# Forty-two matmuls whose result nobody reads, put between the attention scores of units 1 to 7

## The chip, the cores and the metric

The kernel runs on one core of one Trainium2 chip. The metric is the device time of one execution in microseconds: the median of repeated runs. Before the change it is 859.24 us, the median of 3 runs (858.91 to 859.52).

## The reference, cut to what matters

Three stages follow each other: attention with a window of 128 keys and 4 sink keys, a feed-forward block with SoLU and layer norm ("moe1"), and a mixture of 8 experts of which each token takes one ("moe2").

```python
# attention: B, H, S, D = 4, 8, 768, 64
scores = np.matmul(q, k.transpose(0, 1, 3, 2)) / np.sqrt(D)
scores = np.where(is_sink | in_window, scores, -1e9)
a = softmax(scores); x = a @ v                    # to 3072 tokens x 512
# moe1: w_in 512x1024, w_out 1024x512
h = x @ w_in; solu = h * softmax(h); ln = layernorm(solu) * g_ln
x = ln @ w_out
# moe2: logits = x @ w_gate; each token goes to its argmax expert e
out = gate * (relu(x @ w1[e]) @ w2[e])
```

## The kernel before, in words

Attention is cut into 32 **units** (n = 0 to 31): two heads by half a sequence each, in three blocks of 128 queries. Line numbers are those of the kernel before. `a_scores(n)` makes six score tiles `s` of 128 x 272 on TensorE (L220 with plain fp32 operands for units 0 to 2, the pair L223 and L224 from unit 3 on). Each is read by VectorE (L226: adds the mask `mk`, takes the row's extreme `mx`) and then by ScalarE (L228: exponential into `P`). After the six, VectorE and GpSimd make the normalised weights `pk`; `a_trans` transposes them on TensorE (L281, tile `tp`), ScalarE copies them out (L282, `pt`), and `a_out` multiplies them with the values (L297 and L303, tile `av`; L308 and L309 copy the result to `bxh` and `bxl`). `a_sinks` handles the sink keys (`skp`).

The weights `w_in` and `w_out` arrive as 64-bit words and are decoded in the first 110 us in 16 **pieces**. A piece is a DMA into `w` on ScalarE's queue, work on VectorE (L329 `dt`, L331 `dec`, L336 `dh`), ScalarE (L332, L334), one add on GpSimd (L335), and a split into a high and a low part (L344 and L345 for `w_in`: `wih`, `wil`; L373 and L374 for `w_out`). A piece of `w_out` also goes through TensorE (L353 `wt`, L361 `wt2`).

moe1 then takes tiles of 128 tokens: `m_in` makes `h` in two halves of twelve matmuls of 512 columns (L433 to L435), `m_act` applies SoLU and the norm, `m_tr` transposes (`lt`), `m_out` makes `x2` (L498 to L500).

PSUM has eight buffers, in two groups: three for the attention tiles `s`, `tp`, `skp`, `av`, and five for the rest (`h`, `lt`, `x2`, the decode's `dt`, `dh`, `wt`, `wt2` and some more). A buffer is given to a new tile only when the tile before it has been read for the last time. The text of the program gives each step a priority; a scheduler then lays down a fixed order of instructions for each engine, and each engine works through its own order strictly in turn.

Of the kernel before, what the change touches and what calls it, by code (L numbers as in the profile page):

```python
# [10 lines left out]
BF16 = mybir.dt.bfloat16  # L11
# [19 lines left out]
WB, DB, EB, NXR, XGB = 3, 4, 2, 2, 6  # L31
PA = 3
NATP = 3
KLV = 2
HWP = 3
LA = 2
# [12 lines left out]
def raw(ap):  # L49
    return ap.bitcast(F32)  # L50
# [3 lines left out]
def body(ctx, tc, a):  # L54
    nc = tc.nc
    V, A, G, T, SY = nc.vector, nc.scalar, nc.gpsimd, nc.tensor, nc.sync
    qT, kx, vp, vk = a["qT"], a["kx"], a["vp"], a["vk"]

    const = ctx.enter_context(tc.tile_pool(name="const", bufs=1))
# [18 lines left out]
    def ps(name):  # L78
        if name in ATT:
            a_ = True  # L80
        elif name in MOE:
            a_ = False
        else:
            flip[0] += 1
            a_ = flip[0] % 8 < PA
        return ps_p.tile([128, 512], F32, tag="psa" if a_ else "psm", name=name, bufs=PA if a_ else 8 - PA)

    ATT, MOE, flip = ("s", "tp", "skp", "av"), ("h", "lt", "x2", "wt", "wt2", "rk", "dt", "dh"), [0]


    ident = const.tile([128, 128], F32, name="ident")
# [2 lines left out]
                    pattern=[[-1, 128]], channel_multiplier=1)  # L94
    ones = at.tile([128, 128], F32, tag="pk", name="ones", bufs=PKB)
    V.memset(ones, 1.0)

    bm = const.tile([128, 4], F32, name="bm")
    G.affine_select(out=bm, in_=ones[:, 0:4], compare_op=ALU.is_ge, fill=0.0, base=0,
# [23 lines left out]
    mkb = at.tile([128, 3, 272], BF16, name="mk")  # L123
# [35 lines left out]
    def unit(n):  # L159
        b, c = divmod(n, H)  # L160
        return b, c // 4, c % 4

    def a_load(n):
        b, hf, j = unit(n)
        nat = n < NATP
        qd = at.tile([128, 384], F32, tag="qA" if nat else "qd", name="qd", bufs=QKB)
# [9 lines left out]
    def a_split(n):  # L176
# [9 lines left out]
        A.activation(out=qA, in_=qd, func=AF.Copy)  # L186
        (V if n < KLV else G).tensor_tensor(out=kl, in0=kd, in1=raw(kA), op=ALU.subtract)
        G.tensor_tensor(out=lA, in0=qd, in1=raw(qA), op=ALU.subtract)  # L188
# [17 lines left out]
    def a_scores(n, mid=()):  # L206

        b, hf, j = unit(n)
# [3 lines left out]
        for i in range(3):  # L212
            for r in range(2):
                rows = slice(64 * r, 64 * r + 64)
                s = ps("s")
                c0 = 144 * max(3 * hf + i - 1, 0) - KB[hf]
                qs, ks = slice(128 * i, 128 * i + 128), slice(c0, c0 + 272)
                if n < NATP:
                    q, k = qk_t[n][r]
                    T.matmul(s[:, 0:272], q[rows, qs], k[rows, ks], start=True, stop=True)  # L220
                else:
                    q, ql, k = qk_t[n][r]
                    T.matmul(s[:, 0:272], q[:, qs], k[:, ks], start=True, stop=False)  # L223
                    T.matmul(s[:, 0:272], ql[:, qs], k[:, ks], start=False, stop=True)  # L224
                cc = slice(3 * r + i, 3 * r + i + 1)
                V.tensor_tensor_reduce(out=P[:, r, i, :], in0=s[:, 0:272], in1=mkb[:, min(3 * hf + i, 2), :],  # L226
                                       scale=-0.125, scalar=3.0e38, op0=ALU.add, op1=ALU.min, accum_out=mx[:, cc])
                A.activation(out=P[:, r, i, :], in_=P[:, r, i, :], func=AF.Exp, scale=-1.0, bias=mx[:, cc],  # L228
                             accum_out=sm[:, cc])
                yield 0.45 if n < NATP else 0.23  # L230
            if i == 1:
                yield from mid
# [115 lines left out]
    def load_w_out():  # L348
# [20 lines left out]
        for k in range(8):  # L369
# [11 lines left out]
            if last:  # L381
# [7 lines left out]
    tri = const.tile([128, 128], BF16, name="tri")  # L389
    G.affine_select(out=tri, in_=ones, compare_op=ALU.is_gt, fill=0.0, base=0, pattern=[[1, 128]],  # L390
                    channel_multiplier=-1)
    ones_b = const.tile([128, 128], BF16, name="ones_b")
    V.memset(ones_b, 1.0)
    acc = const.tile([128, NE], BF16, name="acc")
    V.memset(acc, 0.0)
    iot8 = const.tile([128, NE], F32, name="iot8")
# [273 lines left out]
    wt, xe_t, ht_t, ev_t = {}, {}, {}, {}  # L670
# [546 lines left out]
```

## Time and profile before

| what | value |
|---|---|
| median of 3 runs | 859.24 us |
| the profiled execution, own time | 864.54 us |
| its span | 862.8 us |
| TensorE busy | 796.7 us (92%), 4946 matmuls |
| VectorE, ScalarE, GpSimd busy | 529.1, 487.8, 390.3 us |
| mean granted TensorE clock | 0.974 |

The span runs from the first to the last instruction of the profiled execution; its own time adds 1.7 us around that and is 5.3 us over the median of the runs without a profile. Busy shares are means over stages with different limits: the page's table of 40 slices shows TensorE below 9 tenths in the first five slices (to about 108 us) and again from 500 to 580 us.

### The profile page before, as it was taken

The numbers are of one execution on the slowest core, as the hardware profiler recorded it, in microseconds if no ns is written. First come the engines' busy times: TensorE is split into PE (matmuls) and PEld (weight loads), VectorE is DVE, ScalarE is ACT, GpSimd is POOL, SyncE is SP. The second block draws the span as 40 slices with busy tenths as digits, with TensorE's granted clock in tenths as the row PEclk, the third lists the DMA queues.
The fourth block names the chain that finished last, engine by engine and source line by source line (L and its number), as shares of the span: only waits on it lengthen the run. The fifth ranks groups of instructions, "written<-read, shape, count | busy, mean of one in ns | idle before, by whom it ended". The sixth has DMA issues, their size and how long they took to land.

```text
span 862.8 us, 15228 instructions
## 1 busy us (share of the span) xinstructions
PE 796.7 (92%) x4946; PEld 693.4 (80%) x4946; DVE 529.1 (61%) x1781; ACT 487.8 (57%) x1206; POOL 390.3 (45%) x412
## 2 busy tenths in 40 slices
PE   2577899999999999999999978689999999999996
PEld 1256778879888988888888878679988888989886
DVE  7976778867898878898775665315323332435431
ACT  5787768777767867677764442126324243435541
POOL 4776745363545454635441044135334353525532
PEclk9996799999999999999999989979999999999999
DMA  8677555576665566465330081265525344536420
GB/s 261 191 200 202 137 131 140 91 127 162 117 135 111 140 167 112 116 148 151 78 51 13 14 249 36 67 217 174 173 81 171 102 135 146 164 120 203 129 85 17
DMA packets 77384, 113.56 MB, mean 132 GB/s; under 512 B 15149, under 2 KB 53485, under 8 KB 77296
## 3 DMA queue, kind: packets, MB, share of 16 engines
q1 hardware_dynamic: 69744, 90.24, 41.3%
q0 software_dynamic: 5248, 13.88, 4.5%
q10 hardware_dynamic: 2304, 8.39, 3.2%
q8 instruction: 41, 0.67, 0.3%
q14 instruction: 47, 0.39, 0.2%
HBM read 71.44 MB, written 13.94 MB: 99 GB/s over the span
## 4 chain that ended last, share of the span: by engine, by line
PE 68%; DMA 14%; DVE 7%; issue 5%; ACT 3%; POOL 1%; SPq 1%; POOLq 0%; ACTq 0%; DVEq 0%
PE y L789 5%; PE y L787 5%; PE y L788 5%; PE ht L767 5%; PE ht L768 5%; PE ht L769 5%; PE x L498 4%; PE h L435 4%; PE h L434 4%; PE h L433 4%; PE x L500 4%; PE av L303 4%; PE x L499 4%; DMA id_d<-tok_i,si 4%; DMA w<-w_out 3%
## 5 line engine op out<-in xcount | busy, mean ns | idle before, releaser
L228 ACT ACTIVATE P<-P,mx 128x272 f32<-128x272 f32 x192 | 99.1, 518 | 41.7 <-DVE mx L226 39.4
L498 PE MATMUL x<-woh,lh 128*128 128x260 f32 x384 | 112.8, 294 | 0.4 <-DVE ll L483 0.4
L500 PE MATMUL x<-woh,ll 128*128 128x260 f32 x384 | 110.3, 288 | 0.0
L499 PE MATMUL x<-wol,lh 128*128 128x260 f32 x384 | 110.0, 287 | 0.0
L698 POOL TENSOR_TENSOR wl<-wst,wh 128x1024 fp32r<-128x1024 f32 x30 | 72.1, 2405 | 71.5 <-ACT wh L697 71.3
L226 DVE CUSTOM_DVE_ANT_0 P<-s,mk 128x272 f32<-128x272 f32 x192 | 81.0, 434 | 21.0 <-PE s L224 18.1
L769 PE MATMUL ht<-xeh,wl 128*128 128x288 f32 (+6 forms) x288 | 90.3, 314 | 0.0
L768 PE MATMUL ht<-xel,wh 128*128 128x288 f32 (+6 forms) x288 | 90.3, 314 | 0.0
L697 ACT ACTIVATE wh<-wst 128x1024 fp32r<-128x1024 f32 x58 | 61.5, 1061 | 50.7 <-PE ht L768 36.3
L787 PE MATMUL y<-wh,hh 128*128 128x512 f32 x224 | 90.1, 403 | 0.0
L767 PE MATMUL ht<-xeh,wh 128*128 128x288 f32 (+6 forms) x288 | 89.4, 314 | 0.0
L789 PE MATMUL y<-wh,hl 128*128 128x512 f32 x224 | 88.2, 395 | 0.0
L788 PE MATMUL y<-wl,hh 128*128 128x512 f32 x224 | 88.0, 394 | 0.0
L433 PE MATMUL h<-wih,bxh 128*128 128x512 f32 x192 | 78.2, 407 | 0.0
L435 PE MATMUL h<-wih,bxl 128*128 128x512 f32 x192 | 76.6, 400 | 0.0
L434 PE MATMUL h<-wil,bxh 128*128 128x512 f32 x192 | 76.3, 397 | 0.0
L498 PEld LDWEIGHTS x<-woh,lh 128*128 128x128 f32 x384 | 73.3, 191 | 2.7 <-issue 1.4
L771 DVE SCALAR_TENSOR_TENSOR hl<-ht,hh 128x288 fp32r<-128x288 f32 (+6 forms) x80 | 38.5, 492 | 59.8 <-ACT hh L770 59.4
L188 POOL TENSOR_TENSOR lA<-qd,qA 128x384 fp32r<-128x384 f32 x29 | 29.4, 1013 | 99.9 <-ACT qA L186 98.8
L698 DVE TENSOR_TENSOR wl<-wst,wh 128x1024 fp32r<-128x1024 f32 x28 | 43.8, 1566 | 49.4 <-ACT wh L697 49.4
L499 PEld LDWEIGHTS x<-wol,lh 128*128 128x128 f32 x384 | 73.2, 191 | 1.0 <-issue 0.3
L500 PEld LDWEIGHTS x<-woh,ll 128*128 128x128 f32 x384 | 73.1, 191 | 0.6 <-issue 0.5
(235 smaller groups left out, 2134.9 us busy)
## 6 DMA issues: line engine op xcount, KB each, us to landing
wst<-w SPq DMA_DIRECT2D x64, 512.0 KB
x_d<-xrow SPq DMA_DIRECT2D x24, 264.0 KB
qd<-qT SPq DMA_DIRECT2D x32, 192.0 KB
qB<-qA SPq DMA_DIRECT2D x58, 96.0 KB
lB<-lA SPq DMA_DIRECT2D x58, 96.0 KB
kd<-kx SPq DMA_DIRECT2D x16, 280.0 KB
w<-w_in ACTq DMA_DIRECT2D x8, 512.0 KB
w<-w_out ACTq DMA_DIRECT2D x8, 512.0 KB
```

The costliest lines, as they stand in the source:

```text
L433: T.matmul(h, xh[k], wih[:, k, cs], start=(k == 0), stop=False)
L435: T.matmul(h, xl[k], wih[:, k, cs], start=False, stop=(k == 3))
L498: T.matmul(p[:, 0:HW], lh[:, k, :], woh[:, k, c, :], start=(k == 0), stop=False)
L499: T.matmul(p[:, 0:HW], lh[:, k, :], wol[:, k, c, :], start=False, stop=False)
L500: mm = T.matmul(p[:, 0:HW], ll[:, k, :], woh[:, k, c, :], start=False, stop=(k == 7))
L698: last_l[c % 2] = (G if c % 2 else V).tensor_tensor(out=l_, in0=st, in1=raw(h_), op=ALU.subtract)
L767: T.matmul(o, wh[:, k, fs], xh(k), start=(k == 0), stop=False)
L768: T.matmul(o, wh[:, k, fs], xl(k), start=False, stop=False)
L769: T.matmul(o, wl[:, k, fs], xh(k), start=False, stop=(k == 3))
L787: T.matmul(o, hh[:, k, sl], wh, start=(k == 0), stop=False)
L788: T.matmul(o, hh[:, k, sl], wl, start=False, stop=False)
L789: T.matmul(o, hl[:, k, sl], wh, start=False, stop=(k == 7))
```

## The change

After each pair of VectorE and ScalarE instructions on a score tile, in units 1 to 7, one matmul is issued: 128 x 128 ones (bf16) times the first 512 columns of the bf16 mask tile, into a new PSUM tile `fill` that nothing reads. That is 42 matmuls, each with its own load of the ones. `fill` belongs to the PSUM group of five that the decode and moe1 use. The tile of ones, which other steps use already, is made earlier in the text. Nothing else in the text changes, but the scheduler lays down a new order for every engine.

```diff
--- before.py
+++ after.py
@@ -31,6 +31,7 @@
 WB, DB, EB, NXR, XGB = 3, 4, 2, 2, 6
 PA = 3
 NATP = 3
+NFILL = 8
 KLV = 2
 HWP = 3
 LA = 2
@@ -85,7 +86,7 @@
             a_ = flip[0] % 8 < PA
         return ps_p.tile([128, 512], F32, tag="psa" if a_ else "psm", name=name, bufs=PA if a_ else 8 - PA)
 
-    ATT, MOE, flip = ("s", "tp", "skp", "av"), ("h", "lt", "x2", "wt", "wt2", "rk", "dt", "dh"), [0]
+    ATT, MOE, flip = ("s", "tp", "skp", "av"), ("h", "lt", "x2", "wt", "wt2", "rk", "dt", "dh", "fill"), [0]
 
 
     ident = const.tile([128, 128], F32, name="ident")
@@ -94,6 +95,8 @@
                     pattern=[[-1, 128]], channel_multiplier=1)
     ones = at.tile([128, 128], F32, tag="pk", name="ones", bufs=PKB)
     V.memset(ones, 1.0)
+    ones_b = const.tile([128, 128], BF16, name="ones_b")
+    V.memset(ones_b, 1.0)
 
     bm = const.tile([128, 4], F32, name="bm")
     G.affine_select(out=bm, in_=ones[:, 0:4], compare_op=ALU.is_ge, fill=0.0, base=0,
@@ -227,6 +230,8 @@
                                        scale=-0.125, scalar=3.0e38, op0=ALU.add, op1=ALU.min, accum_out=mx[:, cc])
                 A.activation(out=P[:, r, i, :], in_=P[:, r, i, :], func=AF.Exp, scale=-1.0, bias=mx[:, cc],
                              accum_out=sm[:, cc])
+                if 0 < n < NFILL:
+                    T.matmul(ps("fill"), ones_b, mkb.rearrange("p a b -> p (a b)")[:, 0:512], start=True, stop=True)
                 yield 0.45 if n < NATP else 0.23
             if i == 1:
                 yield from mid
@@ -389,8 +394,6 @@
     tri = const.tile([128, 128], BF16, name="tri")
     G.affine_select(out=tri, in_=ones, compare_op=ALU.is_gt, fill=0.0, base=0, pattern=[[1, 128]],
                     channel_multiplier=-1)
-    ones_b = const.tile([128, 128], BF16, name="ones_b")
-    V.memset(ones_b, 1.0)
     acc = const.tile([128, NE], BF16, name="acc")
     V.memset(acc, 0.0)
     iot8 = const.tile([128, NE], F32, name="iot8")
```

Three places show what the scheduler made of it. In the changed kernel the lines are 1 to 5 higher (L226 becomes L229, L329 becomes L334).

The first is VectorE's order from the second half of the mask's making up to the first score tile's reading. Before, with the three `dt`, `dh` and `dec` rows of the second and third decode pieces in it (one more, `dt_297`, stands four rows ahead of these); `mk_100` is the finished mask:

```order
L331 SCALAR_TENSOR_TENSOR dec_296<-w64_294,dt_297 128x512
L145 SCALAR_TENSOR_TENSOR mkf_103<-rel_102,mkf_103 128x816
L336 SCALAR_TENSOR_TENSOR dh_242<-dh_242,dec_237 128x512
L575 TENSOR_SCALAR flag_165<-par_95,flag_165 128x1
L329 TENSOR_SCALAR dt_355<-w64_352 128x512
L150 SCALAR_TENSOR_TENSOR mkf_103<-mkf_103,kid_104 128x3x16
L336 SCALAR_TENSOR_TENSOR dh_301<-dh_301,dec_296 128x512
L576 TENSOR_SCALAR flag_165<-par_95,flag_165 128x1
L331 SCALAR_TENSOR_TENSOR dec_354<-w64_352,dt_355 128x512
L256 CAST vhl_366<-vkd_262 128x64
L152 TENSOR_SCALAR mk_100<-mkf_103 128x816
```

The same stretch now, from the mask's first step to the first score tile (L229, tile `s_211`):

```order
L147 TENSOR_SCALAR mkf_105<-rel_104,par_97 128x816
L152 TENSOR_SCALAR kid_106<-kid_106,par_97 128x48
L577 TENSOR_SCALAR flag_165<-par_97 128x1
L148 SCALAR_TENSOR_TENSOR mkf_105<-rel_104,mkf_105 128x816
L578 TENSOR_SCALAR flag_165<-par_97,flag_165 128x1
L341 SCALAR_TENSOR_TENSOR dh_242<-dh_242,dec_237 128x512
L153 SCALAR_TENSOR_TENSOR mkf_105<-mkf_105,kid_106 128x3x16
L579 TENSOR_SCALAR flag_165<-par_97,flag_165 128x1
L155 TENSOR_SCALAR mk_102<-mkf_105 128x816
L580 TENSOR_SCALAR flag_165<-flag_165 128x1
L350 TENSOR_TENSOR wil_68<-dh_242,wih_67 128x512
L229 ISA P_208,mx_209<-s_211,mk_102 128x272
```

Five instructions of the second and third piece have left the place ahead of the mask, and one `wil` has left the place behind it; they stand later, behind scores. The second piece's `dt` (now `dt_309`) waits for `fill_277`, which holds the buffer before it, and that fill waits for the mask.

The second is TensorE's order at the end of unit 0 (`s_211` to `s_231`) and the start of unit 1. Before:

```order
L220 MATMUL s_219<-kd_201,qd_200 128x272
L220 MATMUL s_223<-kd_201,qd_200 128x272
L220 MATMUL s_227<-kd_201,qd_200 128x272
L220 MATMUL s_231<-kd_201,qd_200 128x272
L220 MATMUL s_267<-kd_205,qd_204 128x272
```

Now, with `fill_295` as the fifth fill in a row behind the third score of unit 0:

```order
L234 MATMUL fill_295<-mk_102,ones_b_84 128x512
L223 MATMUL s_223<-kd_201,qd_200 128x272
L223 MATMUL s_227<-kd_201,qd_200 128x272
L234 LDWEIGHTS ones_b_84
L234 MATMUL fill_301<-mk_102,ones_b_84 128x512
L223 MATMUL s_231<-kd_201,qd_200 128x272
```

Fills stand between the scores of a unit ahead of the one that they belong to. Of the 42, 33 stand ahead of the first score of unit 3; 3 stand in unit 4, and 6 in unit 5, and none later. Twelve of them wait for VectorE: one for the mask, eleven for the end of a decode step that holds their buffer.

The third is TensorE's order at the start of the second half of moe1's first tile (`h_1371` before, `h_1455` now; `wt2` is the decode's last step). Before, the scores ahead of it are those of unit 8, four of six:

```order
L361 MATMUL wt2_1297<-wg_sb_123,xt_1285 128x8 x4
L353 MATMUL wt_1304<-ident_77,dec_1271 128x128 x4
L223 MATMUL s_1154<-kB_1082,qB_1078 128x272
L224 MATMUL s_1154<-kB_1082,lB_1080 128x272
L223 MATMUL s_1159<-kA_1081,qA_1077 128x272
L224 MATMUL s_1159<-kA_1081,lA_1079 128x272
L223 MATMUL s_1164<-kB_1082,qB_1078 128x272
L224 MATMUL s_1164<-kB_1082,lB_1080 128x272
L361 MATMUL wt2_1311<-wg_sb_123,xt_1309 128x8 x4
L433 MATMUL h_1371<-wih_67,bxh_448 128x512
L434 MATMUL h_1371<-wil_68,bxh_448 128x512
```

Now all six scores of unit 8 and of unit 9 are ahead of it, and the last four of these are those of unit 9:

```order
L366 MATMUL wt2_1381<-wg_sb_125,xt_1369 128x8 x4
L358 MATMUL wt_1388<-ident_77,dec_1355 128x128 x4
L226 MATMUL s_1435<-kA_1324,qA_1320 128x272
L227 MATMUL s_1435<-kA_1324,lA_1322 128x272
L226 MATMUL s_1443<-kB_1325,qB_1321 128x272
L227 MATMUL s_1443<-kB_1325,lB_1323 128x272
L226 MATMUL s_1448<-kA_1324,qA_1320 128x272
L227 MATMUL s_1448<-kA_1324,lA_1322 128x272
L226 MATMUL s_1459<-kB_1325,qB_1321 128x272
L227 MATMUL s_1459<-kB_1325,lB_1323 128x272
L366 MATMUL wt2_1395<-wg_sb_125,xt_1393 128x8 x4
L436 MATMUL h_1455<-wih_67,bxh_472 128x512
```

Ahead of this place the changed order has done eight more score pairs, two more `tp`, one more `av` and one more `skp` than the order before. From here on attention stays about one unit ahead of moe1, until both orders meet again at moe1's end.

## Rows read from the trace of the kernel before

**Rows 1.** windows: stretch, length, busy time (instructions) of each engine, granted clock, DMA share, GB/s.

```profile
10.00:44.00 34.00, 18.54 (x45) 9.41 (x45) 34.00 (x89) 23.64 (x59) 19.59 (x19) 1.00 0.76 227
...
60.00:104.00 44.00, 34.59 (x190) 28.95 (x190) 31.89 (x97) 33.48 (x89) 29.51 (x32) 0.73 0.68 179
...
140.00:500.00 360.00, 357.98 (x2542) 314.93 (x2541) 281.05 (x1121) 253.85 (x721) 158.30 (x172) 1.00 0.50 108
```

**Rows 2.** windows, five stretches that alternate between the two clock levels.

```profile
58.00:64.60 6.60, 4.28 (x33) 3.15 (x32) 4.60 (x15) 5.25 (x17) 5.88 (x7) 0.99 0.82 207
64.60:71.40 6.80, 6.41 (x29) 5.83 (x31) 5.59 (x15) 6.04 (x16) 3.96 (x5) 0.51 0.83 229
...
75.00:81.80 6.80, 6.40 (x29) 6.07 (x30) 4.06 (x16) 4.70 (x12) 3.09 (x4) 0.52 0.78 227
81.80:88.50 6.70, 4.85 (x38) 3.62 (x35) 4.86 (x15) 6.70 (x20) 6.53 (x6) 0.99 0.76 192
88.50:98.70 10.20, 9.15 (x45) 7.43 (x44) 6.36 (x20) 7.38 (x20) 7.30 (x10) 0.51 0.41 101
```

**Rows 3.** timeline of TensorE: start, duration, engine, line, operation, out<-in, partitions, type.

```profile
55.52 0.43 PE L224 MATMUL s<-kB,lB 128*128 128x272 f32 x1
...
60.70 0.29 PE L224 MATMUL s<-kA,lA 128*128 128x272 f32 x1
```

**Rows 4.** timeline of VectorE at the start of attention.

```profile
16.21 0.68 DVE L345 TENSOR_TENSOR wil<-dh,wih 128x512 fp32r<-128x512 f32 x1
16.81 0.22 DVE L257 TENSOR_TENSOR vhl<-vkd,vhl 128x64 fp32r<-128x64 f32 x1
16.94 0.43 DVE L226 CUSTOM_DVE_ANT_0 P<-s,mk 128x272 f32<-128x272 f32 x1
```

**Rows 5.** timeline of GpSimd, one add of the decode.

```profile
21.06 1.28 POOL L335 TENSOR_TENSOR dec<-dec,w 128x512 int32<-128x512 int32 x1 [4.29 <-ACT wih L344]
```

**Rows 6.** lines of ScalarE, 60 to 104 us: count, busy time, mean duration, idle before.

```profile
L228 ACT ACTIVATE P<-P,mx 128x272 f32<-128x272 f32 x23 | 11.9, 521 | 2.2 <-DVE mx L226 1.8 <-POOL pt L287 0.5
...
L282 ACT ACTIVATE pt<-tp 128x384 f32<-128x384 f32 x7 | 3.3, 480 | 0.7 <-PE tp L281 0.6
...
L185 ACT ACTIVATE kA<-kd 128x560 fp32r<-128x560 f32 (+1 forms) x4 | 2.4, 610 | 1.6 <-PE s L224 1.6
L186 ACT ACTIVATE qA<-qd 128x384 fp32r<-128x384 f32 x4 | 2.1, 519 | 0.0
...
L308 ACT ACTIVATE bxh<-av 128x384 fp32r<-128x384 f32 x4 | 2.0, 490 | 2.3 <-PE av L303 2.3
```

**Rows 7.** timeline of TensorE from 104 to 122 us.

```profile
106.72 0.59 PE L297 MATMUL av<-skt,vsk 128*128 128x384 f32 x2
...
108.70 0.40 PE L223 MATMUL s<-kA,qA 128*128 128x272 f32 x1
...
112.64 0.48 PE L433 MATMUL h<-wih,bxh 128*128 128x512 f32 x1
...
113.19 0.39 PE L435 MATMUL h<-wih,bxl 128*128 128x512 f32 x1
113.42 0.40 PE L433 MATMUL h<-wih,bxh 128*128 128x512 f32 x1
...
115.61 0.29 PE L223 MATMUL s<-kA,qA 128*128 128x272 f32 x1
...
115.86 0.40 PE L435 MATMUL h<-wih,bxl 128*128 128x512 f32 x1
...
120.99 0.82 PE L281 MATMUL tp<-ident,pk 128*128 128x128 f32 x6
121.56 0.60 PE L297 MATMUL av<-skt,vsk 128*128 128x384 f32 x2
```

**Rows 8.** waits, 60 to 112 us: of VectorE, and of ScalarE.

```profile
DVE P L226 <- PE s L224: 7.0, 4, 3.8
...
ACT w L332 <- DMA w<-w_out: 3.6, 1, 3.6
```

## The prediction

> **What bounds the kernel now.** I read the windows first, then the waits, then the rows of the stretch that the change touches. From 140 to 500 us TensorE is busy for 357.98 of 360 us at full granted clock [rows 1]. Nothing added or saved on another engine matters there: the time of this part is the sum of TensorE's work. So the whole question is at what moment TensorE becomes saturated, and how much of its work is done by then. That moment is the start of the second half of moe1's first tile, at 112.64 us [rows 7]. Ahead of it there are two regimes. From 10 to 44 us VectorE is busy for 34.00 of 34 us and TensorE for 18.54 [rows 1]: 15.5 us of TensorE are free. From 60 to 104 us no engine is full: ScalarE 33.48 of 44 us, VectorE 31.89, TensorE 34.59 at a mean granted clock of 0.73 [rows 1]. There TensorE swings between its two levels: at 2.4 GHz it is busy for 4.28 of 6.6 and 4.85 of 6.7 us, and each time it then falls to 1.2 GHz (means of 0.51 and 0.52, the edges of the stretches included), is busy for 6.41 of 6.8, 6.40 of 6.8 and 9.15 of 10.2 us, and rises again [rows 2]. That makes about 24 us at the low level. One more thing is to be read here: the column says 1.00 ahead of 58 us, but the second matmul of a score pair takes 0.43 us at 55.52 and 0.29 at 60.70 [rows 3]. By the durations TensorE is at the low level until about 57 us, and the column shows nothing of it.
>
> **The fills themselves.** The tile of ones is VectorE's second step in both orders, so its earlier place in the text costs nothing. The trace has no such matmul. The nearest are the 512-column matmuls of moe1, 0.23 us from start to start at the high level [rows 7]; twice that, 0.46, is the bound for the low one, whose clock is half. So 42 fills are 9.7 to 19.3 us of TensorE. Were each on the path, the kernel would be slower by that. But 33 of them stand ahead of unit 3's scores. They are 7.6 to 15.2 us there, and the 15.5 free us of that stretch cover them: cost 0 there if no score that VectorE is waiting for stands behind one. If that cover is gone, each costs its 0.23 to 0.46. The nine fills of units 4 and 5 (2.1 to 4.1 us) fall into the mixed regime. I take 0 for them, since scores there wait for VectorE and ScalarE as well, and keep 4.1 as the upper end.
>
> **The buffers.** The fills share five PSUM buffers with the decode. In VectorE's order this has moved five decode instructions behind the mask and one `wil` and the two small `vhl` steps behind the first score. A decode step takes 0.60 us (16.21 to 16.81), a `vhl` 0.13 (16.81 to 16.94) [rows 4]: attention starts 6 x 0.60 + 2 x 0.13 = 3.9 us sooner, at about 13.1 instead of 16.94. That is no gain by itself, since VectorE is full and its list is as long as before: the decode is later by what attention is sooner, about one piece, five VectorE steps or 3.0 us. There is one new bubble: with only one piece in flight VectorE reaches `dh_313` after one score, and GpSimd's add in between takes 1.28 us [rows 5]; 1.28 less the score's 0.43 [rows 4] is 0.85. I take 1 us; the lower end is 0, and the upper 3, for eleven fills that wait for a decode step with a score behind them, a quarter of a microsecond each by the cheaper step.
>
> **The order.** At the start of the saturated part the new order has done more: eight score pairs at 0.25 (115.61 to 115.86), two `tp` at 0.57 together (120.99 to 121.56), one `av` at 1.98 (106.72 to 108.70), all from [rows 7], and a `skp` of three transposes, half of the two `tp`, 0.28. Together 4.8 us, which TensorE need not do later: a credit of 4.8. The price is that this is done where TensorE isn't the bound. ScalarE has to do for it eight exponentials at 0.52, two `pt` at 0.48, a `kA` at 0.61, a `qA` at 0.52 and a `bxh` at 0.49 [rows 6], 6.7 us. Were ScalarE full, the start would move by 6.7; were all of it to fall into ScalarE's idle time (10.5 us of 44 [rows 1]), by 0. I take half, 3.4, since that idle time is partly in places that this work can't fill: 3.6 us at once wait for a weight DMA, and VectorE waits 7.0 us for scores [rows 8].
>
> **The clock.** A clock kept high from 60 to 104 us would spare the waits that come from slow scores. Their size is at most VectorE's 7.0 us, the longest of which is 3.8 [rows 8] at the end of the longest low stretch. I take 0, because the fills are in the wrong place: 33 are spent before unit 3, where VectorE is the bound whatever TensorE's clock, none stands behind unit 5, and the long low stretch from 88.5 to 98.7 us belongs to units 6 and 7. The lower end is 5: 3.8, and a third of the rest. The rule that speaks for the change is in the Trainium skill, TensorE: Matmul & The Clock Gate, section Part 1: The HAM clock gate: throttled is the default, and activity releases it. The rows on the alternation agree [rows 2]; by that rule alone the sum would be 5 lower. The same page, section A second HAM failure mode: psum-queue depth-cycling, speaks against it: matmuls that cycle through PSUM buffers with small idle gaps between groups leave the clock swinging. No run here shows a fill yet; by it the term stays 0.
>
> **The sum.** 0 for the fills, 1.0 for the bubble, 3.4 for the unit moved ahead, 4.8 credit, 0 for the clock: 0.4 us faster. The sum is made against the profiled span of 862.8 us (862.4 after). Its execution took 864.54, 5.3 us above the median of the runs, and this distance I carry over: 859.24 - 0.4 = 858.8 us. A measurement here can tell about 0.2%, 1.7 us.
>
> **Rivals.** First, slower: the decode becomes what TensorE waits for. Its last step, `wt2`, stands right ahead of the saturated part in both orders. If the 3.0 us by which the decode starts later last until there, and ScalarE is full (6.7), the sum is 3.0 + 6.7 - 4.8 = 4.9 slower, 864.1 us. For it speaks that ScalarE and VectorE are at three quarters in the mixed stretch and that the decode is serial through its buffers; against it, that 10.5 us of idle ScalarE time can absorb such a delay. It decides as soon as the second half of the first `h` starts later than 112.64 + 4.8 = 117.4 us. With all upper ends (4.1 + 3 + 6.7 - 4.8) it is 9.0, 868.2 us. Second, faster: the clock stays at the high level through units 4 to 7, and the waits for scores go: 0.4 + 5 = 5.4 faster, 853.8 us. For it: the low level alone makes pairs of scores last 1.5 times as long [rows 3]; against it: where the fills stand. Third, the attention lead is real and the price small: if ScalarE's added 6.7 us fit wholly into idle time and there is no bubble, it is 4.8 faster, 854.4 us. That the change does nothing at all can be excluded only for its result: the orders of all engines differ to moe1's end.
>
> **How the numbers follow.** I give 0.42 to the forecast case, in which terms of both signs cancel to within 3 us; 0.28 to the slower rival; 0.16 to the clock and 0.12 to the cheap attention lead; 0.02 to something else. Of the forecast case's 0.42, which spreads evenly from 855.8 to 861.8, the part below 857.5 is 0.12, the part within 1.7 us of the old median 0.24, the part above 861 is 0.06. So faster 0.40, same 0.24, slower 0.35, and the odd 0.01 goes to the last. The forecast case's own range is 855.8 to 861.8; the 8-in-10 range takes in the centres of the rivals, 852.5 to 865.5, and leaves out the far ends of both.
>
> **What would show it.** Right: the first score is read near 13 us; VectorE is still full from 10 to 44; the granted clock still falls between 85 and 100 us; the second half of the first `h` starts near 117.0 us (112.64 + 1.0 + 3.4), and at least between 114 and 119; the stretch from there to the end is 4.8 us shorter by TensorE's work. The clock term is wrong if the windows from 60 to 100 show no stretch at 0.5. The bubble term is wrong if VectorE shows waits for TensorE ahead of 44 us of over 3 us. The whole is wrong if TensorE's saturated stretch no longer lasts to 500 us, or if the wait for the routed tokens at 560 to 570 us, after moe1, changes by more than the shift ahead of it.

## The result and the profile after

The changed kernel takes 872.17 us (median of 4 runs, 868.51 to 874.07) against 859.38 us of the kernel before beside it: a ratio of 1.0144, 95% interval 1.0104 to 1.0183, so 1.4% slower, 12.8 us. The profiled execution took 874.07 us, its span is 872.3 us (before 862.8).

Windows of the changed kernel, columns as in [rows 1], the same three stretches:

```profile
10.00:44.00 34.00, 29.15 (x69) 11.00 (x69) 29.36 (x82) 20.11 (x52) 15.81 (x17) 1.00 0.61 182
60.00:104.00 44.00, 34.06 (x168) 27.05 (x171) 27.68 (x80) 32.01 (x86) 28.09 (x31) 0.69 0.70 179
140.00:500.00 360.00, 357.71 (x2532) 314.20 (x2531) 280.96 (x1111) 256.87 (x729) 154.54 (x171) 1.00 0.50 108
```

The saturated part is as full as before (357.71 of 360 us). Ahead of it VectorE is no longer full: 29.36 us of 34 where it had 34.00, and 27.68 of 44 where it had 31.89. ScalarE and GpSimd do less there too. The loss is ahead of the saturated part, and on these three engines it is idle time, not work. TensorE has more to do there, 29.15 us of 34 where it had 18.54: the fills.

Timeline of TensorE at the start of that part, columns as in [rows 7]:

```profile
128.13 0.95 PE L366 MATMUL wt<-wg_sb,xt 128*128 128x8 f32 x8
128.94 0.48 PE L436 MATMUL h<-wih,bxh 128*128 128x512 f32 x1
```

The second half of the first `h` starts at 128.94 us, 16.3 later than in [rows 7], directly behind the decode's last `wt2`. So what TensorE waits for is the decode. It was late from the start. The loads of its weights, one 512 KB piece each, in the view of the tile `w` (line, queue or engine, operation, tile, count, least, median and longest duration in ns, start of the first and last), and `wol`, the step that ends a piece of `w_out`; of the kernel before:

```profile
L325 ACTq DMA_DIRECT2D w<-w_in x8: 334/342/453, 0.8 to 25.4; - x8
L325 ACTq DMA_DIRECT2D w<-w_out x8: 334/334/370, 29.8 to 77.9; - x8
L374 DVE SCALAR_TENSOR_TENSOR wol<-dh,g_sb,woh x8: 705/744/754, 47.0 to 105.9; 128x512 fp32r<-128x512 f32 x8
```

and of the changed kernel:

```profile
L330 ACTq DMA_DIRECT2D w<-w_in x8: 335/350/453, 0.8 to 38.4; - x8
L330 ACTq DMA_DIRECT2D w<-w_out x8: 334/335/368, 39.7 to 90.8; - x8
L379 DVE SCALAR_TENSOR_TENSOR wol<-dh,g_sb,woh x8: 708/744/751, 58.5 to 120.9; 128x512 fp32r<-128x512 f32 x8
```

The last load of `w_in` is issued 13.0 us later, the first piece of `w_out` ends 11.5 us later, the last 15.0. The fifth load is the first late one (18.8 us, before 13.5). How a fill makes the sixth later still is seen on ScalarE, which issues these loads in its own order (timeline, idle time ahead and what ended it in brackets):

```profile
23.35 0.62 ACT L339 ACTIVATE dh<-w 128x512 f32<-128x512 f32 x1
...
27.33 0.64 ACT L339 ACTIVATE dh<-w 128x512 f32<-128x512 f32 x1 [2.82 <-PE fill L234]
27.41 0.34 ACTq L330 DMA_DIRECT2D w<-w_in  x1
...
31.12 0.67 ACT L337 ACTIVATE w<-w 128x512 int32<-128x512 uint32 x1 [1.61 <-DMA w<-w_in]
...
32.54 0.57 ACT L349 ACTIVATE wih<-dh 128x512 fp32r<-128x512 f32 x1
```

and VectorE's step behind it:

```profile
33.14 0.69 DVE L350 TENSOR_TENSOR wil<-dh,wih 128x512 fp32r<-128x512 f32 x1 [2.40 <-ACT wih L349]
```

The `dh` at 27.33 needs a PSUM buffer that a fill held; ScalarE stood 2.82 us. The next load comes 0.08 us after it (before, the sixth load was issued at 16.8 us, here at 27.4). ScalarE's next decode step needs that load and waits 1.61 us; behind it in ScalarE's order stands the `wih` of an earlier piece, and VectorE idles 2.40 us for that. The chain of waits shows the same (start, length, what):

```profile
12.71 0.49 DVE mk L155
13.28 2.27 PE fill L234 x5
15.55 1.21 PE s L223 x4
16.76 0.54 PE fill L234
...
26.32 0.98 PE fill L234 x2
27.41 3.68 DMA w<-w_in
...
39.67 6.73 DMA w<-w_out
...
55.36 4.11 DMA w<-w_out
...
69.37 6.49 DMA w<-w_out
```

From 13 to 27 us the fills and the slow scores of unit 0 and 1 are the chain, in a stretch where TensorE was not on it before. Behind that it runs through the loads of `w_out`, as it did before from 29.8 us on.

### The profile page after: what moved, and what is told of

Read it like the earlier page. It is cut to its first block, busy times and chain, and to the rows that moved or that the text cites. A ratio compares the mean times of both kernels' runs of the same rounds, so it can differ in the third digit from the quotient of the medians.

```text
span 872.3 us, 15319 instructions
## 1 busy us (share of the span) xinstructions
PE 813.8 (93%) x4986; PEld 695.8 (80%) x4988; DVE 528.3 (61%) x1781; ACT 488.2 (56%) x1206; POOL 386.0 (44%) x412
## 4 chain that ended last, share of the span: by engine, by line
PE 77%; DMA 10%; DVE 5%; issue 4%; ACT 2%; POOL 1%; POOLq 0%; SPq 0%; ACTq 0%; DVEq 0%
PE h L436 5%; PE h L438 5%; PE h L437 5%; PE x L501 5%; PE y L790 5%; PE y L792 5%; PE y L791 5%; PE ht L770 5%; PE x L503 5%; PE ht L772 5%; PE ht L771 5%; PE x L502 5%; PE av L308 4%; DMA w<-w_out 3%; PE s L226 3%
## 5 line engine op out<-in xcount | busy, mean ns | idle before, releaser
L229 DVE CUSTOM_DVE_ANT_0 P<-s,mk 128x272 f32<-128x272 f32 x192 | 80.3, 434 | 23.9 <-PE s L227 22.1
L191 POOL TENSOR_TENSOR lA<-qd,qA 128x384 fp32r<-128x384 f32 x29 | 29.3, 1011 | 103.6 <-ACT qA L189 103.6
L701 DVE TENSOR_TENSOR wl<-wst,wh 128x1024 fp32r<-128x1024 f32 x28 | 43.9, 1566 | 49.4 <-ACT wh L700 49.4
```

## The experiments

The numbers of all profiled executions, read from their traces. **Start** is that of the second half of the first `h`; **scores** those of attention that stand ahead of it in TensorE's order; **moe1** runs from there to the end of the last `x2`, the **tail** from there to the end of the span; **low** is the time at the lower clock level between 58 and 112 us. Ratios are to runs of the kernel before beside them on the same chip (its medians there lay between 855.9 and 862.1 us). The profiled execution is one of several, and its own time can lie far from the kernel's median: 5.0 us above it in e5, 6.0 in e3, 6.1 in e4 and 7.1 in e10, 5.8 below it in e6 and 7.8 in e14. Differences of that size between two rows of the table show little by themselves.

| kernel | scores | last w_in load | first wol | start | moe1 | tail | low | ratio [95%] |
|---|---|---|---|---|---|---|---|---|
| before | 52 | 25.4 | 47.0 | 112.6 | 423.0 | 327.2 | 23.9 | 1 |
| e11 before, again | 52 | 25.1 | 46.5 | 108.5 | 418.0 | 325.2 | 14.6 | 0.9989 [0.9965, 1.0014] |
| after | 60 | 38.4 | 58.5 | 128.9 | 415.0 | 328.4 | 28.4 | 1.0144 [1.0104, 1.0183] |
| e15 after, again | 60 | 38.0 | 59.0 | 126.8 | 412.8 | 328.0 | 26.7 | 1.0114 [1.0090, 1.0138] |
| e1 units 1 to 3 | 52 | 38.6 | 56.1 | 120.2 | 427.2 | 327.9 | 33.5 | 1.0158 [1.0101, 1.0215] |
| e2 8 columns | 54 | 34.5 | 53.1 | 115.9 | 424.8 | 328.4 | 23.9 | 1.0083 [1.0026, 1.0140] |
| e3 in the score's tile | 49 | 25.4 | 46.8 | 111.4 | 433.2 | 329.6 | 17.1 | 1.0095 [1.0023, 1.0168] |
| e4 kept in place | 66 | 48.9 | 83.7 | 147.3 | 418.1 | 327.6 | 26.7 | 1.0321 [1.0251, 1.0390] |
| e5 no fill, one dt later | 55 | 33.4 | 49.7 | 120.1 | 423.9 | 326.2 | 27.3 | 1.0113 [1.0080, 1.0146] |
| e6 no fill, nine dt later | 55 | 32.6 | 52.7 | 118.5 | 418.7 | 325.7 | 23.9 | 1.0155 [1.0107, 1.0203] |
| e7 own buffer | 49 | 25.4 | 47.2 | 109.6 | 442.5 | 321.0 | 17.1 | 1.0194 [1.0141, 1.0247] |
| e8 attention's buffers | 45 | 25.3 | 45.9 | 101.1 | 432.5 | 326.3 | 6.8 | 1.0053 [1.0028, 1.0078] |
| e9 as e8, units 4 to 7 | 51 | 25.2 | 46.3 | 110.2 | 425.0 | 327.7 | 13.6 | 1.0084 [1.0051, 1.0116] |
| e10 as e3, units 4 to 7 | 48 | 25.2 | 46.5 | 103.8 | 435.0 | 327.6 | 10.2 | 1.0068 [1.0039, 1.0097] |
| e12 no fill, 4 buffers | 48 | 25.2 | 47.9 | 107.0 | 441.1 | 322.9 | 23.9 | 1.0193 [1.0151, 1.0235] |
| e13 decode issued early | 54 | 25.1 | 47.7 | 116.7 | 418.2 | 326.7 | 20.5 | 1.0085 [1.0065, 1.0104] |
| e14 unit 1 only | 54 | 29.3 | 48.6 | 110.8 | 412.5 | 328.8 | 23.9 | 1.0077 [1.0041, 1.0114] |

**Which part of the fills costs: e1 to e4.** The theories at this point were the order (one attention unit more stands ahead of `h`), the buffers shared with the decode, and the fills' run time.

e1, fewer units:

```diff
-NFILL = 8
+NFILL = 4
```

> The added products go only between the scores of the second to the fourth unit (18 of 42 stay, 512 columns each). In the written order, the first h of the mixture then stands where it stood before: its second half right behind the score 8.3, not 9.5. Theory of the order (one more attention unit stands ahead of the first h, and that alone costs the time): 859 us, the same as before, and the second half of the first h starts within 2 us of 112.6. Theory of the buffers (each added product holds one of the five PSUM buffers that the decode also uses): 18/42 of the 12.8 us stay, 864.8. Theory of the run time (each added product costs TensorE what it runs): also 18/42, 864.8, but with the second half of the first h late by 5 us in place of 16.

874.99 us, 1.6% slower: as slow as the change, with 18 of 42 fills and with the order at `h` as it was before. None of the three theories predicted it; the two that go by the number of fills left 18/42 of the loss. First `wol` is at 56.1, start at 120.2, so most of the lag comes from the fills ahead of unit 3. moe1 adds another 4.2 to 9.2 us to it.

e2, the same fills, 8 columns wide:

```diff
-T.matmul(ps("fill"), ones_b, mkb.rearrange("p a b -> p (a b)")[:, 0:512], start=True, stop=True)
+T.matmul(ps("fill")[:, 0:8], ones_b, mkb.rearrange("p a b -> p (a b)")[:, 0:8], start=True, stop=True)
```

> All 42 added products stay and each still takes a PSUM buffer of the decode's group of five, but each is 8 columns wide in place of 512. The second half of the first h stands behind the score 8.5 (before 8.3, after 9.5). Theory of the order: 859 to 861 us. Theory of the buffers: as much as the change, 872, since every buffer is taken and given back as there. Theory of the run time: 42 products of about 0.06 us instead of 0.22 to 0.43: 859 to 860. If the time is near 872 the buffers are it; if near 859 they are not.

868.57 us, 0.8% slower, between the expectations. Fills of almost no length still delay the first `wol` by 6 us; with their length it is 5 us more (58.5 in the change). Neither theory holds alone.

e3, no buffer of their own (240 columns, into the unused part of the score's tile):

```diff
-T.matmul(ps("fill"), ones_b, mkb.rearrange("p a b -> p (a b)")[:, 0:512], start=True, stop=True)
+T.matmul(s[:, 272:512], ones_b, mkb.rearrange("p a b -> p (a b)")[:, 0:240], start=True, stop=True, skip_group_check=True)
```

> All 42 added products stay, 240 columns each, but write into columns 272 to 511 of the score's own PSUM tile, so that none takes a buffer of its own. The second half of the first h stands behind the score 8.0. Theory of the order: the order at the first h is a little earlier than before, 857 to 859 us. Theory of the buffers: 859, no buffer is taken. Theory of the run time: 240/512 of the 12.8 us stay, 865. Clock: if a TensorE kept busier holds its clock up to 112 us and that is worth what the trace of before lost there, 854 to 856.

Loads, first `wol` and start are those of before: without shared buffers there is no lag. Yet it is 0.95% slower, and in the profiled execution, the slowest of its four, the loss is in moe1. In the waits of TensorE, 140 to 500 us, stands what the first profile of before shows once, for 1.5 us:

```profile
PE s L227 <- DMA lA<-lA: 6.7, 4, 4.1
```

Scores of moe1's time wait for a copy (`lA`, on SP's queue), the longest of them 4.1 us, from 226 us on; right behind it the clock falls (windows):

```profile
229.30:236.00 6.70, 5.83 (x18) 4.97 (x19) 2.57 (x7) 2.08 (x6) 0.00 (x0) 0.50 0.47 114
```

e4, every fill kept at its place in the text:

```diff
-T.matmul(ps("fill"), ones_b, mkb.rearrange("p a b -> p (a b)")[:, 0:512], start=True, stop=True)
+tc.keep_in_program_order(T.matmul(ps("fill"), ones_b, mkb.rearrange("p a b -> p (a b)")[:, 0:512], start=True, stop=True))
```

> As the change, but each added product is kept at its place in the program, right behind its score, instead of where the scheduler lets it slip; same 42 products of 512 columns, same five shared buffers. The first h now stands even later: its second half behind the score 10.5 (before 8.3, after 9.5). Theory of the order: about one unit later than the change, which is 12.8 us for one unit so 872 + 8 to 13 = 880 to 885 us. Theory of the buffers: as many buffers taken as in the change, 872 give or take 2. Theory of the run time: the same 42 products, 872.

888.75 us, 3.2% slower. The order theory put the size about right (26.7 us measured, 20 to 26 expected), but the first `wol` is at 83.7 us, 37 later than before: the `h` stands later in the order because the decode ends later.

**The lag without a fill, and the fills without the lag: e5 to e8.** The new theory: the change is slow because the decode's second piece is put behind the fills, and every later load and step follows it. e5 and e6 take the kernel before and queue the `dt` of one piece, or of nine, behind the scores where the change put them; nothing else is asked of the scheduler, which lays down a new order all the same:

```diff
...
+    GATE, sr, np_ = {2: 2}, [], [0]
...
-        V.tensor_scalar(out=t0, in0=hi, scalar1=0x07FFFFFF, scalar2=3, op0=ALU.bitwise_and,
-                        op1=ALU.logical_shift_left)
+        np_[0] += 1
+        g_ = GATE.get(np_[0])
+        with (tc.issue_after(sr[g_]) if g_ is not None else ExitStack()):
+            V.tensor_scalar(out=t0, in0=hi, scalar1=0x07FFFFFF, scalar2=3, op0=ALU.bitwise_and,
+                            op1=ALU.logical_shift_left)
```

`sr` lists the instructions that read scores (its filling is left out here); in e6 the table is `{2: 2, 3: 5, 4: 7, 5: 9, 6: 11, 7: 11, 8: 15, 9: 17, 10: 17}`, piece to score.

> The kernel before, without any added product, but VectorE's first step of the second decode piece (dt) is queued behind the third score's reading of unit 0, where the change put it. Nothing else is asked of the order; in the written order the last piece then ends behind the score 9.0 (before 8.3) and the second half of the first h stands there too. Theory of the decode's lag (the change is slow because the decode starts a piece later and every later step follows it): the first step wol of w_out at 53 us instead of 47.0, the second half of the first h at 116 to 122, 863 to 870 us. Theory of the fills (their run time on TensorE or their wait in it costs the time): there are none here, so 859 to 862, as before.

> The kernel before, without any added product, but the first steps (dt) of the decode pieces 2 to 10 are queued behind the scores where the change put them. Last piece behind the score 9.0. Theory of the decode's lag: first wol at 55 to 58 us (before 47.0, change 58.5), second half of the first h at 120 to 128, 866 to 872 us, nearly all of the change's loss without a single added product. Theory of the fills: as before, 859 to 862.

866.95 and 870.50 us, 1.1% and 1.6% slower, without a single fill: as much as the change. With one VectorE step of 0.6 us queued about 7 us later (15.9 instead of 8.8 us), the kernel takes 10 us more. The way there is not the change's. VectorE stays nearly full (33.16 and 32.83 of 34 us from 10 to 44), and the lag is not simply handed on: in e5 it is 6.7 us at the fifth load, 1.5 at the twelfth, 2.7 at the first `wol` and 7.5 at the start, all against the first profile of before. The starts, at 120.1 and 118.5 us, are not as late as with the change. The profiled execution of e5 was its slowest (871.92 us) and that of e6 its fastest (864.68 us), so they show too much and too little of the loss.

e7 gives the fills a PSUM buffer of their own, kept in place as in e4, and leaves the others four; e12 is the kernel before with four (the last line alone, without the fills):

```diff
+        if name == "fill":
+            return ps_p.tile([128, 512], F32, tag="psf", name=name, bufs=1)
-        return ps_p.tile([128, 512], F32, tag="psa" if a_ else "psm", name=name, bufs=PA if a_ else 8 - PA)
+        return ps_p.tile([128, 512], F32, tag="psa" if a_ else "psm", name=name, bufs=PA if a_ else 7 - PA)
...
```

> All 42 added products of 512 columns, kept right behind their scores, but in a PSUM buffer of their own, so that the decode and moe1 keep four buffers that no added product ever holds. In the written order the decode's second and third piece stand ahead of the mask again, and the second half of the first h behind the score 8.0. Theory of the decode's lag: first wol at 47 to 49 us, second half of the first h within 4 us of 112.6, 857 to 864 us. Theory of the fills' run time: 42 products as in the change, 872. Theory of the clock: if a busier TensorE holds its clock, less than the 24 us at the low level between 58 and 112 us, and up to 5 us off the time.

> The kernel before without any added product, but with four PSUM buffers instead of five for the decode and moe1, as in the run where the added products had a buffer of their own. Theory that the four buffers made that run slow: 868 to 875 here too, with the second half of the first h near 112 and the loss in moe1, whose tiles then follow each other later. Theory that its added products did: 857 to 861.

874.83 and 872.80 us, both 1.9% slower. With 42 fills of full length in place the loads and the start are those of before (109.6), so the fills' run time isn't the loss. What e7 loses, e12 loses without a fill: it is the missing fifth buffer. moe1 takes 441.1 instead of 418.0 to 423.0 us, and the waits of TensorE in e12, 140 to 500 us, have a row that neither trace of before has:

```profile
PE x L498 <- DVE r L530: 3.8, 8, 1.2
```

Eight times `x2` waits for a VectorE step, 3.8 us in all; the rest of the 20 us was not followed up.

e8 puts the fills into attention's three buffers:

```diff
-    ATT, MOE, flip = ("s", "tp", "skp", "av"), ("h", "lt", "x2", "wt", "wt2", "rk", "dt", "dh", "fill"), [0]
+    ATT, MOE, flip = ("s", "tp", "skp", "av", "fill"), ("h", "lt", "x2", "wt", "wt2", "rk", "dt", "dh"), [0]
```

> All 42 added products of 512 columns, but each takes one of the three PSUM buffers of attention instead of the decode's five. The decode is then never behind an added product; attention is. In the written order the decode ends early against attention: the second half of the first h behind the score 7.2 (before 8.3). Theory of the decode's lag: second half of the first h at 108 to 113 us, and with one unit of attention less done by then (a debit of about 5 us later) 859 to 865. Theory of the fills' run time: 872. Theory that what counts is attention's place: attention is later here, so slower by as much, 865 or more.

861.43 us, 0.5% slower, with a start 7 to 12 us sooner than before. Here the clock does what the second rival had from the fills, windows:

```profile
64.70:71.50 6.80, 6.68 (x26) 4.96 (x26) 4.56 (x15) 4.60 (x12) 3.17 (x6) 0.50 0.76 194
71.50:119.30 47.80, 43.95 (x277) 33.30 (x275) 34.77 (x108) 33.30 (x92) 28.10 (x31) 1.00 0.57 150
```

TensorE is busy for 92% of 47.8 us and stays at 2.4 GHz. But seven scores fewer are done at the start, attention is now the late one (moe1 waits 1.9 us for `bxh` at 357 us), and moe1 takes 432.5 us. TensorE is busy for 417.0 of them and idle for 15.6; before it was busy for 411.8 and 410.5 and idle for 11.2 and 7.5.

**Fills only where the clock swings: e9 and e10**, units 4 to 7, in attention's buffers (the other line of e8) or in the score's tile (that of e3); the first 44 us keep the order of before.

```diff
-                if 0 < n < NFILL:
+                if 3 < n < 8:
```

> Added products of 512 columns only between the scores of units 4 to 7 (24 of them), each in one of attention's three PSUM buffers. The first 44 us keep the order of before, and the second half of the first h stands behind the score 8.2 (before 8.3). Theory of the decode's lag with the clock (added products in the place where TensorE swings between its levels keep it high, and nothing of the decode is late): under 14 us at the low level between 58 and 112 us (before 24), second half of the first h at 106 to 111 us, time 2 to 6 us under that of before. Theory that the clock is worth nothing: within 2 us of before. Theory of the fills' run time: 24/42 of 12.8 us slower, +7.

> Added products of 240 columns in units 4 to 7 (24 of them), each written into columns 272 to 511 of the score's own PSUM tile, so that no buffer is taken. The first 44 us keep the order of before; the second half of the first h stands behind the score 7.5, four scores sooner than before. Theory of the decode's lag with the clock: under 18 us at the low level between 58 and 112 us, second half of the first h at 103 to 109 us; less about 1 us for the four scores that are then still to do, 2 to 5 us under the time of before. Theory that the clock is worth nothing: 0 to 2 us over that of before. Theory of the fills' run time: +3.

863.41 and 861.07 us, 0.8% and 0.7% slower; the expected gain did not come. The low time falls to 13.6 and 10.2 us, and e10 starts at 103.8. But e9's start is inside what the kernel before reaches by itself (108.5 to 112.6), and its low time just under (14.6 in e11). e10, with four scores fewer done, needs 435.0 us for moe1 in a profiled execution that is 7.1 us above its median, so that figure is too high for the kernel.

**How much one execution tells: e11 and e15**, both kernels unchanged.

> The kernel before, unchanged, once more, to see how one execution of it differs from another. Theory: up to the second half of the first h (112.6 us in the first profile) executions agree within 1.5 us, and what makes them 852 to 866 us long comes after 140 us, from single waits of TensorE for the copies of lA and the lower clock behind them (first profile: 1.5 us at 192).

> The change itself, unchanged, once more, to see how much of its late start belongs to one execution. Theory of the decode's lag: the loads of weights are again 5 us (fifth) to 10 us (eighth and later) behind those of before, the first wol at 57 to 60 us, the second half of the first h at 124 to 130, whatever the clock's swings do. Theory that the first profile caught an unlucky execution: second half of the first h under 120.

The expectation for e11 was wrong: two executions of one program differ by 4.1 us already at the start (108.5 and 112.6), with the lower level for 14.6 and 23.9 us. Windows of e11, beside the second row of [rows 1]:

```profile
60.00:104.00 44.00, 36.35 (x217) 29.08 (x219) 35.58 (x104) 36.07 (x96) 32.88 (x34) 0.84 0.73 193
```

So a difference in start below some 4 us says nothing. The change repeats: its loads, its first `wol` (59.0) and its start (126.8) agree with the first profile within 2.2 us. VectorE's busy time from 10 to 44 us repeats as well: 29.36 and 29.69 us in the change, 34.00 in both executions of before. From 60 to 104 us the ranges meet, 27.68 and 31.38 us against 31.89 and 35.58.

**The change with the decode issued early: e13; six fills: e14.** The text hands out PSUM buffers in its own order. e13 issues the decode's pieces sooner in the text, so that they get their buffers ahead of the fills:

```diff
-C0, C1, WSTEP, WSTEP2, RATIO = 110, 62, 6, 2, 0.7
+C0, C1, WSTEP, WSTEP2, RATIO = 110, 20, 2, 2, 0.7
```

> The change with all its 42 added products of 512 columns in the same five buffers, but the text issues a decode piece after every second step of attention instead of every sixth (and those of w_out from step 20 instead of 62), so that the early pieces are given their PSUM buffers ahead of the added products. In the written order the second and third piece stand ahead of the mask again and the first wol behind the score 2.5, as before the change; the second half of the first h stands behind 8.5. Theory of the decode's lag (the added products only hurt because they take buffers ahead of the decode's second piece): loads of weights issued at the old times (the fifth at 13.5 us, not 18.8), first wol near 47, second half of the first h at 108 to 116, 857 to 865 us. Theory that 42 products in shared buffers cost their time wherever they stand: 870 to 874.

862.39 us, 0.85% slower, where the change beside it has 865.69 us. All 42 fills are left, of full length and in the same five buffers, and the lag is gone: loads and first `wol` (47.7) are on time, and the last piece's `wol` is even sooner than before (97.8 us against 105.9 and 101.7). What remains comes behind it: 22 fills now stand between the scores of unit 7 and 8, ahead of the last `wt2`, and the start is 116.7. Two limits: only 12 of the 42 fills still stand ahead of unit 3 (33 in the change), so e13 moves the fills out of the early stretch as well as serving the early pieces first; and with the lag gone 6.5 of the 9.8 us that the change loses beside it remain. What the earlier decode does to the kernel before, without fills, was not tried.

e14 is the change with `NFILL = 2`.

> The change with the added products of unit 1 alone, 6 of 42. In the written order the second piece stands behind the score 1.0 as with the change, the first wol behind 2.5, the second half of the first h behind 8.5. Theory of the decode's lag: fifth load of weights 4 to 7 us later than before, second half of the first h at 114 to 122, 862 to 870 us although only 6 products are left. Theory of run time or of buffers by number: 6/42 of 12.8 us, 1.8 us over the time of before.

861.76 us, 0.8% slower [0.4, 1.1], with 6 of 42 fills, where their number would make 0.2%. The fifth load is at 18.5 us as in the change; the decode catches up more than expected (the twelfth load at 43.9 us, before 45.3), to a start of 110.8, where 114 to 122 was expected. That is the profiled execution, which was its fastest (854.0). Its loads of `w_out` end where those of before do:

```profile
L330 ACTq DMA_DIRECT2D w<-w_out x8: 334/334/367, 36.4 to 77.2; - x8
```

## Why the prediction was wrong

**Right.** The saturated part is as full as before, so the question was rightly when it starts. The first score is read at 13.79 us (13.1 said). VectorE waits for GpSimd's add once, for 1.1 us (0.85 worked out; the row is below). The clock still falls where it was said to, windows of the changed kernel:

```profile
83.30:90.10 6.80, 4.62 (x31) 2.93 (x29) 5.07 (x13) 5.52 (x17) 5.14 (x5) 0.98 0.68 190
90.10:103.80 13.70, 12.31 (x58) 10.50 (x59) 8.64 (x25) 9.66 (x27) 8.82 (x11) 0.51 0.63 164
```

The credit of 4.8, given as TensorE's work, was right. Windows of moe1, from the start to the end of the last `x2`, of the kernel before and of the change:

```profile
112.64:535.59 422.95, 411.80 (x2890) 362.78 (x2890) 325.89 (x1275) 284.99 (x812) 187.12 (x199) 0.99 0.51 114
128.94:543.93 414.99, 406.49 (x2847) 356.62 (x2847) 321.16 (x1254) 279.45 (x792) 177.56 (x192) 1.00 0.49 112
```

With e11 (410.47) and e15 (405.96) that is 4.9 us less work by the means. The stretch itself is 6.6 us shorter (415.0 and 412.8 instead of 423.0 and 418.0), but the two executions of before alone differ by 5.0.

**Wrong: the start of the saturated part.** The sum had it 4.4 us later (1.0 for the bubble and 3.4 for the unit moved ahead), at 117.0, at most 119. It is at 126.8 to 128.9, 17.3 later by the means of two executions each. 17.3 - 6.6 and 2.0 more in the tail make 12.7 us; 9.8 (e15) and 12.8 were measured. And the measurement told about 0.4%, not the 0.2% that the prediction counted on.

The step that failed is "the decode is later by what attention is sooner, about one piece, five VectorE steps or 3.0 us". In the sum it has no term at all; only the first rival carries the 3.0. It rested on a VectorE that stays full, and so on a delay that is a sum of VectorE steps. In the change VectorE is not full from 10 to 44 us (29.36 of 34 us); it waits, and not for TensorE, which was the sign that the prediction named, but for ScalarE, GpSimd and a load:

```profile
DVE wil L350 <- ACT wih L349: 2.8, 2, 2.4
DVE dh L341 <- POOL dec L340: 1.1, 1, 1.1
DVE dt L334 <- DMA w<-w_in: 0.7, 1, 0.7
```

The delay is one of order, buffers and loads instead. The `dt` of the second piece stands behind a fill, and starts 7.1 us later; the fifth load is 5.3 us late. A `dt` as late makes it late without any fill, by 6.7 us in e5 and 5.6 in e6. A further fill in the decode's PSUM group stands behind slow scores, `dh` waits for it on ScalarE (2.82 us), the load of a later piece stands in ScalarE's order behind `dh`, and with three buffers for the weights each later load waits for a piece three ahead. The sixth load is 10.6 us late in the change, 10.3 in e15 and 10.6 in e1, where this wait is there (2.8, 3.2 and 2.9 us), and 3.5 in e14 and 5.1 in e5, where it is not (e4, whose fifth load is already 13.1 us late, is a case of its own). In the change nothing makes this up: the lag is 13.0 us at the eighth load, 11.5 at the first `wol` and 16 at the start. e5 and e6 show that an order with the decode's early steps later makes the kernel as slow without a fill; e3, e7 and e8 that fills that leave those steps alone don't delay the start; e13 that 42 fills in the same buffers no longer delay a load once the early pieces are served first and most fills stand later.

So it is shown where the late start comes from. How much of the time it costs is less certain, since kernels without any lag (e3, e9) are 0.95% and 0.84% slower too.

The first rival named the mechanism, and its deciding point (117.4 us) was passed, but it had the decode's lag at the same 3.0 us, and so ended at 864.1, at most 868.2. That ScalarE's 10.5 us of idle time can absorb such a delay, which was held against it, failed: from the sixth load to the last the lag is 8.6 to 15.3 us. Why it isn't absorbed stays open. That this idle time is itself the wait for the loads (3.6 us before [rows 8]), so that a later load moves it along, is not borne out. Waits of ScalarE, 60 to 112 us, of the first profile of the change and of e15:

```profile
ACT w L337 <- DMA w<-w_out: 4.2, 3, 2.5
```

```profile
ACT w L337 <- DMA w<-w_out: 0.8, 2, 0.6
```

In e11 it is 1.7 us, so this wait differs as much between two executions as between the two kernels. Nor is it a rule that a lag stays: in e14 it is gone by the twelfth load.

**The fills themselves.** "The 15.5 free us of that stretch cover them: cost 0 there if no score that VectorE is waiting for stands behind one" named its own condition, which did not hold: from 13 to 27 us the fills are on the chain. e2 puts some 5 of the 11.5 us of the first `wol`'s lag on their length; as e2's order differs too, this is no exact share.

**The clock.** The term of 0 holds for this change: 26.7 and 28.4 us at the lower level against 14.6 and 23.9, rather more, partly because the swinging stretch lasts longer. "The fills are in the wrong place" fits the trace: of e15's 42 fills nine run between 58 and 112 us and none behind 83 us, and the lower level from 90.10 to 103.80 us in the change comes with none near it. In e8 24 fills run between 58 and 112 us, and the lower level is down to 6.8 us. This agrees with the Trainium skill, TensorE: Matmul & The Clock Gate, section Part 1: The HAM clock gate (activity releases the throttle). But e7, e9 and e10 have 24 fills there too, and e3 26, with 17.1, 13.6, 10.2 and 17.1 us at the lower level; with one profiled execution each, and 9.3 us between the two of before, only e8's and e10's figures stand clear of those. No run here shows whether the swings are what that page's section A second HAM failure mode: psum-queue depth-cycling describes; the prediction drew on it, but in the change only nine of the 42 fills stand where the clock swings. And the clock was not the prize it was priced at: e8 starts 7 to 12 us sooner and e10 5 to 9, and they end 4.9 and 4.3 us later than the kernel before.

**What stays open.** Every kernel here with another order than before's is 0.5% slower or more, also where the start is on time (e3, e9). In the profiled execution of e3 it is waits for `lA` and the clock behind them. In e9 no single wait of that size is to be found in the saturated part; in moe1 TensorE is busy for 412.6 us and idle for 12.3 (11.2 and 7.5 before). So a part of the change's loss may be what any new order costs here, and no run separates that from the lag: taking the lag away (e13) gave back 3.3 of 9.8 us. No version beat the kernel before.

## What to carry to other kernels

A matmul that nobody reads still takes a buffer, and what the buffer is taken from matters more than its time on the engine: follow the next tile of that group to the engine that waits for it, and from there to every transfer that stands behind it in that engine's order. Where loads run a fixed number of buffers ahead, don't count on idle time later to absorb a delay of the first pieces: the change carried 9 to 15 us of it from the sixth load to the last, though with six fills (e14) it was made up. Where two streams feed one saturated engine, making one of them sooner pays only as far as the other keeps up: e8 started 7 to 12 us sooner and ended 4.9 us later.

## What the hardware showed unexpectedly

Two executions of the same program differ by 4.1 us after 110 us; TensorE's clock was at 1.2 GHz for 23.9 us in one and for 14.6 us in the other of the 54 us from 58 on. By an estimate from these figures, 9.3 us more at half the clock are 4.7 us less of TensorE's work, about the difference; no run shows that it is the only reason. In e3 one wait of 4.1 us for a DMA, in the saturated part, came with 6.8 us at 1.2 GHz. At half the clock these are 3.4 us less of TensorE's work, so by this estimate the wait cost nearly twice its length.
